# Splitting Q over all rows and queries at once, with DMAs that fill the stationary tiles by halves

## The chip, the cores and the metric

The kernel runs on one core of a Trainium2 chip. The metric is the device time of one execution in microseconds (us); the time of the kernel before is the median of three runs. The engines are TensorE (PE, with its weight loads as PEld), VectorE (DVE), ScalarE (ACT), GpSimd (POOL) and SyncE (SP), which here issues the DMAs. SBUF is the memory on the chip that the engines read, PSUM the one that PE's products land in.

## The reference

```python
# q, k, v: 8 batches, 8 heads, 576 positions, 64 per head
scores = matmul(q, k^T) / 8;  scores = where(pos_q // 64 >= pos_k // 64, scores, -1e9)
attn = exp(scores - rowmax);  attn = attn / (sum(attn) + 1e-9)
x = heads side by side of matmul(attn, v)                       # 8 x 576 x 512
gate = sigmoid(sum over k of conv_w[k] * x shifted by k)        # 5 taps along the positions
x = (gate * (x @ w_val)) @ w_out
u = x + real(fft over positions, then over features of x)
un = (u - mean) / sqrt(var + 1e-6)
out = u + relu(un @ w_ch1) @ w_ch2                              # 512 -> 2048 -> 512
```

Inputs and outputs are 32-bit floats. The change concerns the first line only: the scores of q against k.

## The kernel before

PE multiplies numbers of a shorter format (fp32r). To come near to 32-bit results, an operand is split into two parts: `hi`, the number as a copy into an fp32r tile rounds it, and `lo`, the difference between the number and `hi`. A product is then hi*hi + hi*lo + lo*hi.

The first part of the kernel (about 720 us) does attention, gated convolution and the Fourier mix; the second part (`phase2`, to 1540 us) does the network of 2048 features in nine groups, with weights that DVE decodes at its beginning. The change is in the first part alone. It goes through 32 pairs of heads, four to a batch. The raw tiles `qraw` and `kraw` hold a pair transposed: rows 0 to 63 are the 64 features of head 0, rows 64 to 127 those of head 1, and the 576 columns are positions. A pair has nine score blocks, i = 0 to 8: blocks 0 to 7 are 128 queries of one head (head i mod 2, queries 128 * (i // 2) and on, keys up to there), block 8 is the last 64 queries of both heads at once, in two pieces of 320 and 256 keys.

For blocks 0 to 7 the product needs only two matmuls (L405, L407). The first multiplies a stationary tile that holds q's hi in the 64 rows of the head and q's lo in the other 64 rows (`QQ[p][h]`) with a tile that holds k's hi twice (`KK[p][h]`, copied there by four DMAs of L368): hi*hi + lo*hi in one pass over 128 rows. The second multiplies `QZ`, q's hi with zeros in the other head's rows, with `KL`, k's lo: hi*lo. Block 8 takes three matmuls (mm3) with `QDH` and `QDL`, whose diagonal quarters hold the two heads' last 64 queries.

`split(p)` makes these tiles. Its stages run one to a block, beside the blocks of the pair before: `k_hi` (ACT, L57), then `k_dup` (DMAs, L368), `k_lo` (POOL, L363) and `q_hi` of head 0 (ACT, L63), then `q_lo` of head 0 (DVE, L345, which reads one half of the rows and writes the other) and `q_hi` of head 1, then `q_lo` of head 1 and two `d_hi` (ACT, L351), then two `d_lo` (DVE, L355). `spread(p, g)` copies a half of the queries of each head's hi into `QZ` (L383). The Q and K tiles of a pair are double buffered, `QDH` and `QDL` too; a `QZ` is held once and filled by halves: half 0 (blocks 0 to 3) behind block 4 of the pair before, half 1 (blocks 4 to 7) behind its block 8. The raw tiles come from a pool of three, of which a pair takes two.

After a block's product, DVE takes the row maximum (L427) and ACT the exponential with its sum (L440, `PB`), PE transposes it (L497), ACT copies it out (L502, `PTa`, `PTb`) and PE multiplies with v (L519). Beside that run the convolution's taps and gate (DVE L550, ACT L63), the Fourier products (L158 to L160) and the copies that split their operands. The loop `for n in range(NU + LT + LA)` writes one block per turn, with lags for the steps behind it; a scheduler then reorders the instructions of each engine, and each engine works through its own list in order. All DMAs spoken of here stand in one list, SP's.

Of the kernel before, what the change touches and what calls it, by code (L numbers as in the profile page):

```python
# [17 lines left out]
def kernel(  # L18
# [81 lines left out]
    def phase1():  # L100
        with ExitStack() as c1:
            kp = c1.enter_context(tc.tile_pool(name="kp", bufs=2))
            raw_p = c1.enter_context(tc.tile_pool(name="raw", bufs=3))
            sm = c1.enter_context(tc.tile_pool(name="sm", bufs=6))
            pa = c1.enter_context(tc.tile_pool(name="pa", bufs=1))
            px, pv, pg, pool = (c1.enter_context(tc.tile_pool(name=f"p{n}", bufs=1)) for n in "xvgz")
# [4 lines left out]

            make_identity(nc, ident)

            QDH = [pa.tile([P, P], F32R, name=f"QDH{i}") for i in range(2)]
            QDL = [pa.tile([P, P], F32R, name=f"QDL{i}") for i in range(2)]

            QZ = [[pa.tile([P, 256], F32R, name=f"QZ{h}{g}") for g in range(2)] for h in range(2)]
            PB = [pa.tile([P, 128 * (i // 2 + 1)], F32, name=f"PB{i}") for i in range(NB)]
            PTa = pa.tile([P, 2, 2, 256], F32, name="PTa")
            PTb = pa.tile([P, 2, 5, 320], F32, name="PTb")  # L120
# [184 lines left out]


            NPAIR = B * NP
            qraw, kraw, QQ, KK, KP, KL, VV = {}, {}, {}, {}, {}, {}, {}

            def load(p):  # L310
                if p >= NPAIR:
# [15 lines left out]
            def split(p):  # L327
                if p >= NPAIR:
                    return
                rs = [slice(0, 64), slice(64, 128)]  # L330

                QQ[p] = [kp.tile([P, D], F32R, tag=f"Q{h}", name=f"Q{h}") for h in range(2)]
                KK[p] = [kp.tile([P, S], F32R, tag=f"K{h}", name=f"K{h}") for h in range(2)]
                KP[p] = kp.tile([P, S], F32R, tag="KP", name="KP")
                KL[p] = kp.tile([P, S], F32R, tag="KL", name="KL")
                qq, kk, kh, kl = QQ[p], KK[p], KP[p], KL[p]
                dh, dl = QDH[p % 2], QDL[p % 2]

                def q_hi(h):
                    r = rs[h]  # L340
                    scaled(4, qq[h][r, :], qraw[p][r, 0:D], 0.125)

                def q_lo(h):
                    r = rs[h]
                    nc.vector.scalar_tensor_tensor(  # L345
                        out=qq[h][rs[1 - h], :], in0=qraw[p][r, 0:D], scalar=0.125,
                        in1=qq[h][r, :].bitcast(F32), op0=ALU.mult, op1=ALU.subtract)

                def d_hi(h):
                    r = rs[h]  # L350
                    nc.scalar.activation(out=dh[r, r], in_=qraw[p][r, D:S], func=AF.Copy, scale=0.125)  # L351

                def d_lo(h):
                    r = rs[h]
                    nc.vector.scalar_tensor_tensor(  # L355
                        out=dl[r, r], in0=qraw[p][r, D:S], scalar=0.125,
                        in1=dh[r, r].bitcast(F32), op0=ALU.mult, op1=ALU.subtract)
# [12 lines left out]
                def both(*f):  # L370
                    return lambda: [g() for g in f]

                return Chain(k_hi, both(k_dup, k_lo, lambda: q_hi(0)), both(lambda: q_lo(0), lambda: q_hi(1)),
                             both(lambda: q_lo(1), lambda: d_hi(0), lambda: d_hi(1)),
                             both(lambda: d_lo(0), lambda: d_lo(1)))

            def spread(p, g):

                if p >= NPAIR:
                    return  # L380
                for h in range(2):
                    r = slice(64 * h, 64 * h + 64)
                    nc.sync.dma_start(out=QZ[h][g][r, :].bitcast(F32),  # L383
                                      in_=QQ[p][h][r, 256 * g:256 * g + 256].bitcast(F32))

            sums, scs, maxs = {}, {}, {}

# [2 lines left out]
            def sc_tile(n):  # L390

                sc_at[0] += 1
                if n < NS and sc_at[0] % 5 > 2:
                    return ps_m.tile([P, D], F32, tag="m", name="sc")
                return ps_sc.tile([P, D], F32, tag="sc", name="sc")

            def emit_qk(n):
                p, i = divmod(n, NB)
                if i < 8:

                    h, L = i % 2, P * (i // 2 + 1)
                    w = max(256, L)
                    m = slice(P * (i // 2), P * (i // 2) + P)
                    t = sc_tile(n)
                    nc.tensor.matmul(t[:, 0:w], QQ[p][h][:, m], KK[p][h][:, 0:w], start=True, stop=False)  # L405
                    z = slice(P * (i // 2 % 2), P * (i // 2 % 2) + P)
                    nc.tensor.matmul(t[:, 0:w], QZ[h][i // 4][:, z], KL[p][:, 0:w], start=False, stop=True)  # L407
                    scs[n] = [(t[:, 0:L], 0, L)]
                    return

                sc = []
                for k0, w in ((0, 320), (320, 256)):
                    t = sc_tile(n)
                    mm3(t[:, 0:w], QDH[p % 2], QDL[p % 2], KP[p][:, k0:k0 + w], KL[p][:, k0:k0 + w], True, True)
                    sc.append((t[:, 0:w], k0, w))
                scs[n] = sc

# [412 lines left out]
            prepared = [0]  # L830
            load(0)
            nc.gpsimd.memset(PB[8][:, S:640], 0.0)
            for t in QDH + QDL + QZ[0] + QZ[1]:
                nc.gpsimd.memset(t.bitcast(F32), 0.0)
            split(0).run()
            spread(0, 0)
# [25 lines left out]
            for n in range(NU + LT + LA):  # L862
                if n == N1:
                    now[0] = 0
                p, i = divmod(n, NB)
# [22 lines left out]
                m = n - LT - LA  # L888
# [298 lines left out]
```

## Time and profile before

| | |
|---|---|
| median of 3 runs | 1539.53 us (1539.19 to 1540.07) |
| the profiled execution | 1541.68 us; its span, first to last instruction, 1539.9 |
| PE busy | 1464.1 us (95%), 8300 matmuls |
| DVE busy | 910.4 us (59%), 1894 instructions |
| ACT busy | 696.1 us (45%), 1770 instructions |
| POOL busy | 391.0 us (25%), 352 instructions |
| DMA queue of SP | 23.8% of the 16 engines' span, 108.78 MB |
| granted TensorE clock | 0.987 of full speed |

The busy shares are means over stages with different limits, so they are read by stretch: the first 60 us, the pair loop up to about 650 us, and the second part, in which PE has nearly all of the time. A row that ends in brackets tells how long the engine had stood idle before the instruction, and which instruction released it.

### The profile page before, as it was taken

Reading aid. Unit: us, or ns where it says so; the run is one execution under the profiler, and the core shown is the slowest. Engines: PE = TensorE matmul, PEld = TensorE weight load, DVE = VectorE, ACT = ScalarE, POOL = GpSimd, SP = SyncE. Lnnn points to the kernel's source line nnn. Section 1 sums busy time; section 2 is a strip of 40 time slices with the busy share of each in tenths; the row PEclk is TensorE's granted clock in tenths of the full one; section 3 lists DMA queues with packets and bytes.
Section 4 is the critical chain, followed back from the end, with each engine's and each line's share of the span. In section 5 each row is a group of like instructions: output and inputs, shape, how many; then the busy total and the mean of one; then the engine's idle time right before and its main releaser. Section 6 shows DMA issues by size and latency. Waiting matters only on the chain.

```text
span 1539.9 us, 22720 instructions
## 1 busy us (share of the span) xinstructions
PE 1464.1 (95%) x8300; PEld 1216.1 (79%) x8300; DVE 910.4 (59%) x1894; ACT 696.1 (45%) x1770; POOL 391.0 (25%) x352
## 2 busy tenths in 40 slices
PE   5799999999999999998888999999999999999998
PEld 4567888788888888886667888888888888888887
DVE  8888897979797989779995222222322222322212
ACT  6878777787868686734443211112121211212110
POOL 3433232323232333235434110111111201111100
PEclk9899999999999999999999999999999999999999
DMA  7444343333343433122541001010101001010000
GB/s 219 129 140 125 101 114 93 109 97 105 90 114 93 122 94 99 56 86 92 178 146 68 1 21 35 1 55 1 55 1 52 3 0 55 0 55 1 28 0 28
DMA packets 86624, 110.23 MB, mean 72 GB/s; under 512 B 8944, under 2 KB 60144, under 8 KB 86512
## 3 DMA queue, kind: packets, MB, share of 16 engines
q1 hardware_dynamic: 86512, 108.78, 23.8%
q8 instruction: 65, 1.06, 0.3%
q14 instruction: 47, 0.39, 0.1%
HBM read 62.61 MB, written 18.87 MB: 53 GB/s over the span
## 4 chain that ended last, share of the span: by engine, by line
PE 67%; DVE 20%; issue 6%; ACT 5%; POOL 1%; DMA 1%; SPq 0%; DVEq 0%; ACTq 0%; POOLq 0%
PE o L1079 8%; PE o L1077 8%; PE o L1078 8%; PE psh L1060 8%; PE psh L1059 8%; PE psh L1061 8%; PE av L519 4%; PE pt L497 3%; DVE mx L427 3%; DVE gate L550 2%; PE sc L405 2%; PE psx L158 2%; PE psx L160 2%; DVE st L76 2%; PE psx L159 2%
## 5 line engine op out<-in xcount | busy, mean ns | idle before, releaser
L1065 DVE SCALAR_TENSOR_TENSOR hl<-psh,hh 128x512 fp32r<-128x512 f32 x144 | 99.2, 689 | 397.8 <-ACT hh L1064 397.8
L1064 ACT ACTIVATE hh<-psh 128x512 fp32r<-128x512 f32 x144 | 85.8, 596 | 493.6 <-PE psh L1061 493.6
L1079 PE MATMUL o<-hl,W2H 128*128 128x512 f32 x576 | 226.4, 394 | 17.0 <-DVE hl L1065 17.0
L1061 PE MATMUL psh<-UTH,W1L 128*128 128x512 f32 x576 | 225.1, 391 | 1.2 <-POOL W1L L973 1.1
L1077 PE MATMUL o<-hh,W2H 128*128 128x512 f32 x576 | 225.7, 392 | 0.0
L1078 PE MATMUL o<-hh,W2L 128*128 128x512 f32 x576 | 225.6, 392 | 0.0
L1059 PE MATMUL psh<-UTH,W1H 128*128 128x512 f32 x576 | 224.9, 390 | 0.3 <-ACT W1H L972 0.3
L1060 PE MATMUL psh<-UTL,W1H 128*128 128x512 f32 x576 | 224.5, 390 | 0.0
L440 ACT ACTIVATE PB<-sc,mx 128x128 f32<-128x128 f32 (+4 forms) x320 | 167.2, 525 | 40.7 <-DVE mx L427 35.7
L427 DVE TENSOR_REDUCE mx<-sc 128x1 f32<-128x128 f32 (+4 forms) x320 | 147.9, 473 | 1.9 <-PE sc L160 0.2
L497 PE MATMUL pt<-ident,PB 128*128 128x128 f32 x800 | 140.6, 280 | 5.2 <-ACT XF L474 2.5
L1079 PEld LDWEIGHTS o<-hl,W2H 128*128 128x128 f32 x576 | 108.8, 189 | 44.2 <-DVE hl L1065 21.8
L550 DVE SCALAR_TENSOR_TENSOR gate<-XF,cw,gate 128x575 f32<-128x575 f32 (+3 forms) x128 | 132.5, 1035 | 2.9 <-ACT gate L63 2.1
L1061 PEld LDWEIGHTS psh<-UTH,W1L 128*128 128x128 f32 x576 | 108.4, 188 | 25.2 <-POOL W1L L973 2.5
L1059 PEld LDWEIGHTS psh<-UTH,W1H 128*128 128x128 f32 x576 | 108.6, 189 | 23.5 <-ACT W1H L972 0.7
L1078 PEld LDWEIGHTS o<-hh,W2L 128*128 128x128 f32 x576 | 109.1, 189 | 22.9
L1077 PEld LDWEIGHTS o<-hh,W2H 128*128 128x128 f32 x576 | 108.8, 189 | 22.9 <-ACT hh L1064 0.2
L1060 PEld LDWEIGHTS psh<-UTL,W1H 128*128 128x128 f32 x576 | 108.4, 188 | 22.5
L405 PE MATMUL sc<-K,Q 128*128 128x256 f32 (+2 forms) x256 | 94.5, 372 | 31.9 <-ACT PB L440 21.0
L497 PEld LDWEIGHTS pt<-ident,PB 128*128 128x128 f32 x800 | 100.8, 143 | 18.0 <-ACT PTb L502 9.9
L1088 POOL TENSOR_TENSOR U<-o,U 128x512 f32<-128x512 f32 x32 | 40.3, 1290 | 273.9 <-DVE o L1086 273.9
L502 ACT COPY PTb<-pt 128x512 f32<-128x512 f32 (+1 forms) x192 | 92.2, 500 | 21.7 <-PE pt L497 20.5
(187 smaller groups left out, 3019.2 us busy)
## 6 DMA issues: line engine op xcount, KB each, us to landing
K<-KP SPq DMA_DIRECT2D x128, 144.0 KB, 2.5
rw<-in_w_ch SPq DMA_DIRECT2D x32, 512.0 KB, 3.9
VV<-in_v SPq DMA_DIRECT2D x32, 320.0 KB, 3.3
qraw<-in_q SPq DMA_DIRECT2D x32, 288.0 KB, 3.1
kraw<-in_k SPq DMA_DIRECT2D x32, 288.0 KB, 3.0
out<-U SPq DMA_DIRECT2D x36, 256.0 KB, 2.0
QZ<-Q SPq DMA_DIRECT2D x128, 64.0 KB, 2.2
u_d<-XA SPq DMA_DIRECT2D x16, 289.0 KB, 2.2
```

Of the source, the lines that this page charges most:

```text
L405: nc.tensor.matmul(t[:, 0:w], QQ[p][h][:, m], KK[p][h][:, 0:w], start=True, stop=False)
L427: nc.vector.reduce_max(out=mx[:, j:j + 1], in_=t, axis=AX.X, negate=one)
L440: nc.scalar.activation(out=PB[i][:, k0:k0 + w], in_=t, func=AF.Exp, bias=nm, accum_out=su[:, i + j:i + j + 1])
L497: nc.tensor.transpose(ps[:, j, :], PB[i][:, (j0 + j) * P:(j0 + j + 1) * P], ident)
L550: nc.vector.scalar_tensor_tensor(out=gate[c][:, s:S], in0=XF[:, 0:S - s], scalar=cw[:, c, 4 - s:5 - s], in1=gate[c][:, s:S], op0=ALU.mult, ...
L1059: nc.tensor.matmul(ps, W1H[f][:, c, :], UTH[g][:, c, :], start=(c == 0), stop=False)
L1060: nc.tensor.matmul(ps, W1H[f][:, c, :], UTL[g][:, c, :], start=False, stop=False)
L1061: nc.tensor.matmul(ps, W1L[f][:, c, :], UTH[g][:, c, :], start=False, stop=(c == 3))
L1065: nc.vector.scalar_tensor_tensor(out=l, in0=ps, scalar=0.0, in1=h.bitcast(F32), op0=ALU.max, op1=ALU.subtract)
L1077: nc.tensor.matmul(po[t], W2H[e][:, c], h, start=(e == 0), stop=False)
L1078: nc.tensor.matmul(po[t], W2L[e][:, c], h, start=False, stop=False)
L1079: nc.tensor.matmul(po[t], W2H[e][:, c], l, start=False, stop=(e == NF - 1))
```

## The change

All rows and all 576 columns of `qraw` are split by one ACT instruction (`q_hi`) and one DVE instruction (`q_lo`) into one tile `QHL`, hi in its first half and lo in its second; rows stay where they are. What has to stand in other rows is carried there by DMAs: `q_last` copies the last 64 queries into `QD` (two DMAs), and `spread` fills, per head and half of the queries, `QQ[h][g]`: hi into the first and second 256 columns of the head's rows (one DMA that reads the source twice), lo into the first 256 columns of the other rows (one DMA). `QHL` and `QQ` are held once, and the raw pool has two tiles in place of three. The products read the same numbers as before.

```diff
-            raw_p = c1.enter_context(tc.tile_pool(name="raw", bufs=3))
+            raw_p = c1.enter_context(tc.tile_pool(name="raw", bufs=2))
...
-            QDH = [pa.tile([P, P], F32R, name=f"QDH{i}") for i in range(2)]
-            QDL = [pa.tile([P, P], F32R, name=f"QDL{i}") for i in range(2)]
-            QZ = [[pa.tile([P, 256], F32R, name=f"QZ{h}{g}") for g in range(2)] for h in range(2)]
+            QHL = pa.tile([P, 2, S], F32R, name="QHL")
+            QD = [pa.tile([P, 2, P], F32R, name=f"QD{i}") for i in range(2)]
+            QQ = [[pa.tile([P, 2, 256], F32R, name=f"QQ{h}{g}") for g in range(2)] for h in range(2)]
...
-                QQ[p] = [kp.tile([P, D], F32R, tag=f"Q{h}", name=f"Q{h}") for h in range(2)]
...
-                def q_hi(h):
-                    r = rs[h]
-                    scaled(4, qq[h][r, :], qraw[p][r, 0:D], 0.125)
-                def q_lo(h):
-                    r = rs[h]
-                    nc.vector.scalar_tensor_tensor(
-                        out=qq[h][rs[1 - h], :], in0=qraw[p][r, 0:D], scalar=0.125,
-                        in1=qq[h][r, :].bitcast(F32), op0=ALU.mult, op1=ALU.subtract)
...
+                def q_hi():
+                    nc.scalar.activation(out=QHL[:, 0, :], in_=qraw[p], func=AF.Copy, scale=0.125)
+                def q_lo():
+                    nc.vector.scalar_tensor_tensor(out=QHL[:, 1, :], in0=qraw[p], scalar=0.125,
+                                                   in1=QHL[:, 0, :].bitcast(F32), op0=ALU.mult, op1=ALU.subtract)
+                def q_last():
+                    for r in rs:
+                        nc.sync.dma_start(out=QD[p % 2][r, :, r].bitcast(F32), in_=QHL[r, :, D:S].bitcast(F32))
...
-                return Chain(k_hi, both(k_dup, k_lo, lambda: q_hi(0)), both(lambda: q_lo(0), lambda: q_hi(1)),
-                             both(lambda: q_lo(1), lambda: d_hi(0), lambda: d_hi(1)),
-                             both(lambda: d_lo(0), lambda: d_lo(1)))
+                return Chain(k_hi, both(k_dup, k_lo), wait, q_hi, q_lo, q_last)
             def spread(p, g):
...
+                c = slice(256 * g, 256 * g + 256)
                 for h in range(2):
-                    r = slice(64 * h, 64 * h + 64)
-                    nc.sync.dma_start(out=QZ[h][g][r, :].bitcast(F32),
-                                      in_=QQ[p][h][r, 256 * g:256 * g + 256].bitcast(F32))
+                    nc.sync.dma_start(out=QQ[h][g][rs[h], :, :].bitcast(F32),
+                                      in_=QHL[rs[h], 0:1, c].bitcast(F32).to_broadcast([64, 2, 256]))
+                    nc.sync.dma_start(out=QQ[h][g][rs[1 - h], 0, :].bitcast(F32), in_=QHL[rs[h], 1, c].bitcast(F32))
...
-                    m = slice(P * (i // 2), P * (i // 2) + P)
+                    m = slice(P * (i // 2 % 2), P * (i // 2 % 2) + P)
...
-                    nc.tensor.matmul(t[:, 0:w], QQ[p][h][:, m], KK[p][h][:, 0:w], start=True, stop=False)
-                    nc.tensor.matmul(t[:, 0:w], QZ[h][i // 4][:, z], KL[p][:, 0:w], start=False, stop=True)
+                    q = QQ[h][i // 4]
+                    nc.tensor.matmul(t[:, 0:w], q[:, 0, m], KK[p][h][:, 0:w], start=True, stop=False)
+                    nc.tensor.matmul(t[:, 0:w], q[:, 1, m], KL[p][:, 0:w], start=False, stop=True)
```

(`wait` is a stage that does nothing.) The lines of the kernel after stand some ten to twenty lower in number: L430 is L440 of before, L417 is L427, L492 is L502.

The order of ACT's instructions in the loop, before, at the first pair of a batch: the exponentials of block 7 (`PB_124`) and block 8 (`PB_125`, two pieces) with what stands around them.

```order
L63 ACTIVATE gate_143<-XF_128,cw 128x576
L502 COPY PTa<-pt 128x128
L63 ACTIVATE Q_4863<-qraw 64x512
L440 ACTIVATE PB_124,su<-sc,mx 128x512
L57 CAST KP<-kraw 128x576
L351 ACTIVATE QDH_110<-qraw 64x64
L502 COPY PTa<-pt 128x2x128
L440 ACTIVATE PB_125,su<-sc,mx 128x320
L440 ACTIVATE PB_125,su<-sc,mx 128x256
```

And the same place after, where the two blocks are `PB_123` and `PB_124`.

```order
L63 ACTIVATE gate_142<-XF_127,cw 128x576
L492 COPY PTa<-pt 128x128
L430 ACTIVATE PB_123,su<-sc,mx 128x512
L57 CAST KP<-kraw 128x576
L492 COPY PTa<-pt 128x2x128
L340 ACTIVATE QHL<-qraw 128x576
L430 ACTIVATE PB_124,su<-sc,mx 128x320
L430 ACTIVATE PB_124,su<-sc,mx 128x256
```

The copy of Q ahead of block 7's exponential is gone, and the copy into `QHL` stands ahead of block 8's, with the copy into `QDH` gone.

DVE's order at the same place, before: `XF` is the attention's result, which the convolution's copies on ACT wait for.

```order
L611 TENSOR_TENSOR GL_157<-GF_149,GH_153 128x580
L450 TENSOR_SCALAR su<-su 128x4
L345 SCALAR_TENSOR_TENSOR Q_4862<-qraw,Q_4862 64x512
L540 TENSOR_TENSOR XF_128<-av,XF_128 128x320
L451 RECIPROCAL re<-su 128x4
L588 SCALAR_TENSOR_TENSOR gv_148<-gate_144,psv 128x288
```

And after.

```order
L440 TENSOR_SCALAR su<-su 128x4
L417 TENSOR_REDUCE mx<-sc 128x1
L601 TENSOR_TENSOR GL_156<-GF_148,GH_152 128x580
L441 RECIPROCAL re<-su 128x4
L530 TENSOR_TENSOR XF_127<-av,XF_127 128x320
L578 SCALAR_TENSOR_TENSOR gv_147<-gate_143,psv 128x288
```

The difference for Q no longer stands ahead of `XF`; the short steps on the sums (`su`, `re`) and the convolution's product (`gv`) stand around `XF` as before.

SP's order at the start of the kernel, before, from the copies of pair 0's K on; pair 1's Q was asked for three rows earlier.

```order
L368 DMA K_193<-KP 64x576 x2
L368 DMA K_194<-KP 64x576 x2
L383 DMA QZ_113<-Q_191 64x256
L383 DMA QZ_115<-Q_192 64x256
L383 DMA QZ_114<-Q_191 64x256
L383 DMA QZ_116<-Q_192 64x256
L317 DMA kraw<-in_k 128x576
L234 DMA XA<-in_w_val 128x1024
```

And after, from the same copies on.

```order
L359 DMA K_188<-KP 64x576 x2
L359 DMA K_189<-KP 64x576 x2
L348 DMA QD_110<-QHL 64x2x64 x2
L374 DMA QQ_112<-QHL 64x256
L372 DMA QQ_114<-QHL 64x2x256
L374 DMA QQ_114<-QHL 64x256
L372 DMA QQ_113<-QHL 64x2x256
L374 DMA QQ_113<-QHL 64x256
L372 DMA QQ_115<-QHL 64x2x256
L374 DMA QQ_115<-QHL 64x256
L318 DMA qraw<-in_q 128x576
L320 DMA kraw<-in_k 128x576
```

Pair 1's Q and K are now asked for behind all copies of pair 0's Q.

## Rows read from the trace of the kernel before

**Rows 1.** Busy time by stage (from:to, length, engines busy, clock, DMA, GB/s)

```profile
20.00:60.00 40.00, 29.38 (x158) 20.47 (x158) 37.05 (x85) 29.45 (x82) 19.97 (x22) 0.83 0.59 178
300.00:400.00 100.00, 97.47 (x739) 83.45 (x738) 85.14 (x218) 77.01 (x224) 32.24 (x33) 1.00 0.36 99
760.00:800.00 40.00, 34.70 (x141) 27.09 (x141) 40.00 (x55) 17.95 (x32) 16.27 (x12) 0.96 0.48 155
```

**Rows 2.** PE's waits from 140 to 640 us (total us, times, longest us)

```profile
PE sc L405 <- ACT PB L440: 13.0, 19, 1.4
PE rt L466 <- POOL XF L454: 2.1, 6, 0.4
```

**Rows 3.** Groups by line, whole run (busy us, mean ns, idle before and releaser)

```profile
L550 DVE SCALAR_TENSOR_TENSOR gate<-XF,cw,gate 128x575 f32<-128x575 f32 (+3 forms) x128 | 132.5, 1035 | 2.9 <-ACT gate L63 2.1
...
L345 DVE SCALAR_TENSOR_TENSOR Q<-qraw,Q 64x512 fp32r<-64x512 f32 x64 | 58.3, 910 | 12.2 <-ACT Q L63 10.6
...
L363 POOL TENSOR_TENSOR KL<-kraw,KP 128x576 fp32r<-128x576 f32 x32 | 49.7, 1553 | 47.9 <-ACT KP L57 47.9
...
L63 ACT ACTIVATE Q<-qraw 64x512 fp32r<-64x512 f32 x64 | 40.3, 629 | 11.3 <-PE sc L405 8.1 <-DMA qraw<-in_q 2.5
...
L57 ACT CAST KP<-kraw 128x576 fp32r<-128x576 f32 x32 | 21.7, 679 | 0.1
...
L351 ACT ACTIVATE QDH<-qraw 64x64 fp32r<-64x64 f32 x64 | 16.3, 255 | 0.6
...
L355 DVE SCALAR_TENSOR_TENSOR QDL<-qraw,QDH 64x64 fp32r<-64x64 f32 x64 | 15.4, 241 | 0.8
```

**Rows 4.** Instructions that read qraw: ns shortest/median/longest, and us from first to last

```profile
L345 DVE SCALAR_TENSOR_TENSOR Q<-qraw,Q x64: 684/687/1796, 4.4 to 612.3; 64x512 fp32r<-64x512 f32 x64
```

**Rows 5.** Issues of QZ, 200 to 620 us: ns to issue, us to landing

```profile
L383 SPq DMA_DIRECT2D QZ<-Q x82: 461/462/829, 205.0 to 615.1; - x82
...
DMA to landing us min/median/max: 1.9/2.3/3.7
```

**Rows 6.** Timeline 441 to 447 us: start us, duration us, engine, line, idle before

```profile
441.04 0.69 DVE L345 SCALAR_TENSOR_TENSOR Q<-qraw,Q 64x512 fp32r<-64x512 f32 x1
...
443.81 0.63 ACT L63 ACTIVATE Q<-qraw 64x512 fp32r<-64x512 f32 x1
444.46 0.69 ACT L440 ACTIVATE PB<-sc,mx 128x512 f32<-128x512 f32 x1
...
445.29 0.39 PE L405 MATMUL sc<-K,Q 128*128 128x256 f32 x1 [1.36 <-ACT PB L440]
...
445.85 0.36 ACT L502 COPY PTa<-pt 128x256 f32<-128x256 f32 x1
...
446.31 0.53 ACT L440 ACTIVATE PB<-sc,mx 128x320 f32<-128x320 f32 x1
...
446.99 0.39 PE L405 MATMUL sc<-K,Q 128*128 128x256 f32 x1 [0.17 <-ACT PB L440]
```

**Rows 7.** Timeline 399 to 405 us, another pair

```profile
399.25 0.39 PE L407 MATMUL sc<-KL,QZ 128*128 128x512 f32 x1
...
401.44 0.69 ACT L440 ACTIVATE PB<-sc,mx 128x512 f32<-128x512 f32 x1
...
403.89 0.53 ACT L440 ACTIVATE PB<-sc,mx 128x320 f32<-128x320 f32 x1
...
404.56 0.39 PE L405 MATMUL sc<-K,Q 128*128 128x256 f32 x1 [0.49 <-ACT PB L440]
```

**Rows 8.** Chain of waits at the start: start us, us, what

```profile
24.95 0.70 DVE Q L345
...
26.39 1.80 DVE Q L345
```

**Rows 9.** Timeline of the first 24 us: pair 1's K

```profile
10.24 0.52 SPq L317 DMA_DIRECT2D kraw<-in_k  x1
...
14.71 0.67 ACT L57 CAST KP<-kraw 128x576 fp32r<-128x576 f32 x1
```

More of the change, by code (lines that the diff above doesn't have):

```diff
@@ L307, in phase1 @@
             NPAIR = B * NP
-            qraw, kraw, QQ, KK, KP, KL, VV = {}, {}, {}, {}, {}, {}, {}
+            qraw, kraw, KK, KP, KL, VV = {}, {}, {}, {}, {}, {}
+            rs = [slice(0, 64), slice(64, 128)]
             def load(p):
@@ L329, in split @@
                     return
-                rs = [slice(0, 64), slice(64, 128)]
-                QQ[p] = [kp.tile([P, D], F32R, tag=f"Q{h}", name=f"Q{h}") for h in range(2)]
                 KK[p] = [kp.tile([P, S], F32R, tag=f"K{h}", name=f"K{h}") for h in range(2)]
@@ L335, in split @@
                 KL[p] = kp.tile([P, S], F32R, tag="KL", name="KL")
-                qq, kk, kh, kl = QQ[p], KK[p], KP[p], KL[p]
-                dh, dl = QDH[p % 2], QDL[p % 2]
-                def q_hi(h):
-                    r = rs[h]
-                    scaled(4, qq[h][r, :], qraw[p][r, 0:D], 0.125)
-                def q_lo(h):
-                    r = rs[h]
-                    nc.vector.scalar_tensor_tensor(
-                        out=qq[h][rs[1 - h], :], in0=qraw[p][r, 0:D], scalar=0.125,
-                        in1=qq[h][r, :].bitcast(F32), op0=ALU.mult, op1=ALU.subtract)
[L349 to L357, printed above, removed]
+                kk, kh, kl = KK[p], KP[p], KL[p]
+                def q_hi():
[6 more added lines that the diff above has]
+                        nc.sync.dma_start(out=QD[p % 2][r, :, r].bitcast(F32), in_=QHL[r, :, D:S].bitcast(F32))
                 def k_hi():
@@ L402, in emit_qk @@
                     w = max(256, L)
-                    m = slice(P * (i // 2), P * (i // 2) + P)
+                    m = slice(P * (i // 2 % 2), P * (i // 2 % 2) + P)
                     t = sc_tile(n)
-                    nc.tensor.matmul(t[:, 0:w], QQ[p][h][:, m], KK[p][h][:, 0:w], start=True, stop=False)
-                    z = slice(P * (i // 2 % 2), P * (i // 2 % 2) + P)
-                    nc.tensor.matmul(t[:, 0:w], QZ[h][i // 4][:, z], KL[p][:, 0:w], start=False, stop=True)
+                    q = QQ[h][i // 4]
+                    nc.tensor.matmul(t[:, 0:w], q[:, 0, m], KK[p][h][:, 0:w], start=True, stop=False)
+                    nc.tensor.matmul(t[:, 0:w], q[:, 1, m], KL[p][:, 0:w], start=False, stop=True)
                     scs[n] = [(t[:, 0:L], 0, L)]
@@ L413, in emit_qk @@
                     t = sc_tile(n)
-                    mm3(t[:, 0:w], QDH[p % 2], QDL[p % 2], KP[p][:, k0:k0 + w], KL[p][:, k0:k0 + w], True, True)
+                    mm3(t[:, 0:w], QD[p % 2][:, 0], QD[p % 2][:, 1], KP[p][:, k0:k0 + w], KL[p][:, k0:k0 + w], True, True)
                     sc.append((t[:, 0:w], k0, w))
@@ L832, in phase1 @@
             nc.gpsimd.memset(PB[8][:, S:640], 0.0)
-            for t in QDH + QDL + QZ[0] + QZ[1]:
+            for t in QD + [QQ[h][g][rs[1 - h], 1, :] for h in range(2) for g in range(2)]:
                 nc.gpsimd.memset(t.bitcast(F32), 0.0)
```

## The prediction

> **What bounds the kernel now.** I read the busy time by stage first. From 20 to 60 us TensorE (PE) is busy 29 of 40 us and VectorE (DVE) 37: the start belongs to DVE, which decodes the first weights beside the attention of the first pairs of heads. From 300 to 400 us PE is busy 97.47 of 100 us, DVE 85 and ScalarE (ACT) 77: there PE is the bound, with 2.5% left. From 760 to 800 us DVE is busy all 40 us, decoding the weights of the second part [rows 1]. The reader is to see three stages with two different limits. Next, PE's waits between 140 and 640 us, where the pair loop runs evenly: 13.0 us for an exponential on ACT (nineteen times, the longest 1.4) and 2.1 us for a POOL copy: 15.1 us in 500 [rows 2]. Everything the change can win in the loop is inside that. The 32 pairs are 8 batches of 4; six of the batches fall in these 500 us, so each has some 2.5 us of it. Then I read one such wait event by event, below.
>
> The instruction order of every engine after the last pair's scores is the same in both kernels, and PE and DVE wait for each other there without a gap that the change could use. I take it that whatever is won or lost up to about 640 us is carried unchanged to the end.
>
> **The change, part by part.** PE multiplies the same tiles in the same number; its cost is zero but for waits.
>
> DVE loses, per pair, two differences of 64x512 (L345, mean 910 ns) and two of 64x64 (L355, 241 ns): 2.30 us. It gains one difference of 128x576. No such one stands in the trace with these operands; the nearest are the taps L550, the same operation over 128 partitions and 572 to 575 columns, mean 1035 ns. I take that: 1.27 us less a pair, 40.5 us over 32 pairs [rows 3]. The bounds come from the spread of L345, 684 to 1796 ns [rows 4]: at 0.77 us (684 x 576/512) the pair saves 1.53, at 1.8 us it saves 0.50.
>
> ACT loses two 64x512 copies (629 ns) and two 64x64 (255 ns), 1.77 us, and gains one of 128x576. KP is a copy of that size, 679 ns: 1.09 us less a pair, 35 us in all [rows 3].
>
> That L345 goes from 684 to 1796 ns is in [rows 4]. The Trainium skill, page "SBUF — State Buffer", section "Who interferes with whom", gives a reason: a VectorE instruction with two SBUF inputs and a GpSimd instruction that reads SBUF exclude each other, and the later one waits for the whole of the other. The spread agrees with it. The rule speaks against one long difference: the K difference on POOL (L363, 1553 ns [rows 3]) starts when KP ends, and q_lo comes about 1.06 us later (a PTa copy and q_hi in between), so by that rule up to 0.5 us of each q_lo may be blocked, 16 us of the 40.5. The sum would lose about 1 us by it, as little of that DVE time is on the path.
>
> SP issues 17 DMAs a pair in place of 11. A small one takes 0.462 us [rows 5], so 2.8 us more of a pair's 20 us; the queue has room. Bytes between SBUF tiles grow from 256 to 832 KB a pair, about 29 GB/s on 99, and the DMA share from 0.36 [rows 1] to about 0.47. I cost both at nothing except where something waits for a landing. Three such waits are new. The first product of a pair needs QQ, and its copies are issued behind the products of block 4 of the pair before, five blocks or some 11 us ahead: hidden. QD is read last in a pair: hidden, even were its 256-byte pieces slow. The third is q_hi, which must not overwrite QHL before the second half of the previous pair has been copied out of it. It is queued on ACT in front of the exponentials of the double block (i = 8), for which PE waits. That one counts.
>
> **The loop.** The wait of 1.36 us, once a batch, is in [rows 6]. A DVE difference of Q (441.04, 0.69) stands in front of XF, for which ACT's XH and gate wait; then ACT's own copy of Q (443.81, 0.63) stands in front of the exponential of block 7 (444.46), and PE waits for that one until 445.29. Both are gone in the new order: this exponential comes 0.69 + 0.63 = 1.32 us earlier. But q_hi now stands between it and the exponential of block 8. Before, that one came 446.31 - 445.15 = 1.16 us after block 7's ended; now KP 0.68 + PTa 0.36 + q_hi 0.69 = 1.73 us. It starts at 443.14 + 0.69 + 1.73 = 445.56 in place of 446.31, so the product at 446.99 moves by 0.75 us, not by 1.32: a new wait is late next.
>
> In another pair of the batch PE waits 0.49 us for block 8's exponential at 404.56 [rows 7]. Block 7's products end at 399.64. The later of the two second-half DMAs is issued 0.5 us after that and lands 1.9 to 3.7 us later, 2.3 at the median [rows 5]: at 402.4 with a median landing, at 403.8 with the worst. The exponential of block 7 is 0.6 us earlier without ACT's Q; then its 0.69, KP and PTa put q_hi's turn at 402.6. So it does not wait at the median, and with the worst landing it waits 1.2 us. Before, ACT worked 1.76 us without a gap between the two exponentials (402.13 to 403.89); now KP, a PTa copy or two and q_hi make 1.73 to 2.1 us, after a start 0.6 us earlier. So block 8's exponential stays near 403.5 at the median. I take zero here, between +0.7 (worst landing: q_hi ends at 404.5, not 403.89) and -0.49.
>
> The POOL copy, 2.1 us in six waits or 0.35 a batch, itself follows work in DVE's queue; with a shorter queue I count 0.3 of it. Sum: 1.05 us a batch, and with the uneven batches at the ends 5.2 of them: **-5.5 us**. Bounds: -15 (all the idle time goes) and, as a rival, a loss.
>
> **The start.** Up to 150 us nine pairs are split, 9 x 1.27 = 11.5 us of DVE. How much is on the path? The chain shows 0.70 and 1.80 us for Q at 24.95 and 26.39 [rows 8] for one pair; one new difference costs about 1.04 there: 1.5 us. Some three pairs of the nine have both on the path: -4.5 us, and ACT's share adds 0.5. Against this, pair 1 is loaded later. The raw pool holds two tiles in place of three, so its loads stand on SP behind all copies of pair 0. Its K was issued at 10.24 us and KP began at 14.71 [rows 9]. Now seven more DMAs stand ahead of that K (six more copies of pair 0, and pair 1's own load of Q), at 0.46 us each [rows 5]: K is issued 3.2 us later, at 13.4, and KP follows at about 17.9. The next weight load stands behind it too. In that time DVE has the weights and pair 0 to work on, so about half stays: +1.5 us. Start: **-3.5 us**, between -11.5 (all of DVE's saving counts) and +3 (the whole delay counts and nothing is won).
>
> **The sum** is -9.0 us. The profiled execution took 1541.7 us (span 1539.9 and 1.8 around it), so it would be 1532.7; the median of the runs is 1539.5, 2.2 below it, and there the same saving gives **1530.5 us**.
>
> **Rivals.**
> (a) The relief is hidden. PE is busy 97.5% of the loop, and both engines that are relieved run beside it; if q_hi's new place also eats the 0.75 us, and the late pair 1 eats the start's gain, the rest is within 3 us: 1537 to 1542. For it: the wait that replaces the removed one; against it: DVE's 37 of 40 us at the start.
> (b) Slower: q_hi waits for the copies. Two DMAs, the later one twice the size of QZ, behind a V load; if it lands 3.3 us after its issue, 1 us over the median, q_hi waits from its turn about 0.8 us. From 2.5 us on this decides. Three pairs in four have q_hi in front of block 8; one of the three has slack, so 16 pairs x 0.8 = 13 us are lost, the loop's 5.5 mostly with them (one batch place in two): 1539.5 - 3.5 - 2 + 13 = 1547. For it: the worst landing of 3.7; against: the median of 2.3.
> (c) The start is DVE's alone and the loop's idle time all goes: -11.5 + 1.5 - 11 = -21: 1518. For it: DVE at 93% from 20 to 60 us; against: PE and ACT are busy 29.4 of the 40 us there too [rows 1] and have chains of their own.
> (d) The lower price of a full-width difference does not come, because it is blocked each time at 1.8 us: the pair saves 0.50 us, and the start wins 1.5 instead of 5; with the loop at -4 that is 1535.5.
>
> **Chances.** Forecast 0.48 (1525 to 1536), (d) 0.06, (a) 0.17, (b) 0.19, (c) 0.10. 0.2% is 3.1 us, about what measurements of this kernel tell from no change. Faster by more: the forecast, (c) and most of (d), 0.61; within: (a) and a little of (d), 0.20; slower: (b), 0.19. The range has to leave out at most 0.2: 1519 cuts half of (c), 1545 cuts most of (b), so **1519 to 1545**.
>
> **What would show it.** DVE's Q group at 32 instructions of 0.8 to 1.2 us, some 33 us in all, and ACT's at 0.69. PE's wait for the exponentials in the loop down from 13.0 to about 8 us, with the 1.4 us cases replaced by 0.7 us ones in front of the second product. PE busy from 300 to 400 us above 98.5. The batch shorter by about 1 us. KP of pair 1 at about 18 us. I am wrong if ACT shows q_hi idle before it on a DMA landing by more than 5 us in all (then (b)), if the batch is as long as before (then (a)), or if the stages after 660 us do not keep their length.

## The result, and the profile after

The changed kernel takes 1526.42 us (median of four runs, 1523.36 to 1528.32) against 1539.36: a ratio of 0.9916, 95% interval 0.9897 to 0.9936, or 12.9 us less. A second series gave 0.9908 (0.9895 to 0.9920). The forecast was 1530.5, 9.0 us less. The profiled execution took 1526.26 us, its span 1524.5.

The busy time by stage, columns as in [rows 1]:

```profile
20.00:60.00 40.00, 26.24 (x130) 16.80 (x130) 31.82 (x74) 24.57 (x70) 18.98 (x22) 0.79 0.66 177
300.00:400.00 100.00, 98.62 (x764) 86.57 (x766) 80.59 (x208) 75.78 (x217) 33.65 (x32) 1.00 0.53 137
760.00:800.00 40.00, 34.06 (x139) 26.71 (x138) 40.00 (x54) 17.76 (x32) 17.64 (x14) 0.96 0.40 132
```

PE is up to 98.62 of 100 us in the loop, DVE down by 4.5, ACT by 1.2. The first stage does not look like a gain: every engine is busy less of it than before, PE 26.24 of 40 us in place of 29.38, at a granted clock of 0.79 of full speed in place of 0.83. In the loop the granted clock is 1.00 in both. DMA share in the loop is 0.53, where 0.47 was reckoned.

PE's waits from 140 to 640 us, which answer to [rows 2]:

```profile
PE sc L396 <- ACT PB L430: 8.0, 9, 1.7
```

8.0 us are left of 15.1, so 7.1 us went. But the loop got 13.5 us shorter. The rest is in the waits of PE's weight loads, which no row ahead of the prediction shows. Before:

```profile
PEld sc L405 <- ACT PB L440: 19.0, 27, 1.6
PEld pt L497 <- ACT PTb L502: 6.7, 19, 0.7
...
PEld rt L466 <- POOL XF L454: 4.3, 6, 0.7
...
PEld rt L466 <- POOL KL L363: 1.9, 5, 0.4
```

After:

```profile
PEld sc L396 <- ACT PB L430: 13.0, 18, 1.9
...
PEld pt L487 <- ACT PTb L492: 1.3, 6, 0.2
...
PEld rt L456 <- POOL XF L444: 1.1, 5, 0.2
```

These four waits sum to 31.9 us before and the three to 15.4 after. A weight load that comes late pushes its matmul, but not all of the delay shows as the matmul's idle time. At the place of [rows 6] the weight load shows a longer wait than the 1.36 us of its product:

```profile
445.29 0.19 PEld L405 LDWEIGHTS sc<-K,Q 128*128 128x128 f32 x1 [1.59 <-ACT PB L440]
```

And the product itself is listed with 0.39 us there, with 0.28 where it did not wait (436.46 below). So a part of PE's waiting is counted as busy. From the first product of pair 10 to that of pair 30, with the same matmuls in between, the time fell from 408.7 to 394.9 us: PE's idle time by 5.9 us, its busy time by 7.9 (396.1 to 388.2).

The instructions of the split, with columns as in [rows 3], and the spread of q_lo as in [rows 4]:

```profile
L343 DVE SCALAR_TENSOR_TENSOR QHL<-qraw,QHL 128x576 fp32r<-128x576 f32 x32 | 24.0, 749 | 6.3 <-ACT QHL L340 6.3
...
L340 ACT ACTIVATE QHL<-qraw 128x576 fp32r<-128x576 f32 x32 | 22.2, 694 | 10.9 <-DMA QQ<-QHL 3.2 <-DMA K<-KP 3.1 <-DMA u_d<-XA 2.4
```

```profile
L343 DVE SCALAR_TENSOR_TENSOR QHL<-qraw,QHL x32: 727/748/880, 4.3 to 599.8; 128x576 fp32r<-128x576 f32 x32
```

A full-width difference takes 0.749 us, not 1.035, and none took over 0.88.

Where the time went, by the start of each pair's first product (us, read off the timelines; later kernels below in the same way, as differences from the kernel before):

| | pair 2 | pair 10 | pair 31 | second part's first product | span |
|---|---|---|---|---|---|
| before | 35.98 | 200.06 | 627.40 | 709.3 | 1539.9 |
| changed | +12.8 | +0.2 | -13.3 | -14.8 | -15.4 |
| changed, second series | +11.8 | +0.4 | -12.5 | -15.3 | -16.8 |

So the start gave nothing on balance (pair 2 is late by 12.8 us, pair 10 is level), the loop from pair 10 to 31 gave 13.5 us in 21 pairs, 2.6 a batch, and 2.1 us came behind it, 1.5 of them before the second part. In the loop the step is always at the same place: the first products of pairs 10, 14, 18, 22 and 26 gained 2.0 us each on that of the pair before, that of pair 30 gained 1.8.

The place of [rows 6] once more. First the kernel before, lines that were not shown (columns as there):

```profile
437.65 3.33 POOL L756 TENSOR_TENSOR XA<-XA 128x580 f32<-128x580 f32 x2 [1.50 <-DVE XA L756]
...
438.02 1.67 DVE L611 TENSOR_TENSOR GL<-GF,GH 128x580 fp32r<-128x580 f32 x1
...
439.61 1.40 DVE L450 TENSOR_SCALAR su<-su 128x4 f32<-128x4 f32 x1
...
439.79 0.39 PE L405 MATMUL sc<-K,Q 128*128 128x512 f32 x1
...
441.75 0.49 DVE L540 TENSOR_TENSOR XF<-av,XF 128x320 f32<-128x320 f32 x1
```

And the changed kernel at the same batch:

```profile
430.13 0.15 DVE L440 TENSOR_SCALAR su<-su 128x4 f32<-128x4 f32 x1
...
430.24 3.34 POOL L746 TENSOR_TENSOR XA<-XA 128x580 f32<-128x580 f32 x2 [1.39 <-DVE sc L415]
...
432.29 0.45 DVE L530 TENSOR_TENSOR XF<-av,XF 128x320 f32<-128x320 f32 x1
...
432.48 0.39 PE L396 MATMUL sc<-K,QQ 128*128 128x512 f32 x1
...
434.18 0.69 ACT L430 ACTIVATE PB<-sc,mx 128x512 f32<-128x512 f32 x1
...
436.46 0.28 PE L396 MATMUL sc<-K,QQ 128*128 128x256 f32 x1
...
436.66 0.69 ACT L340 ACTIVATE QHL<-qraw 128x576 fp32r<-128x576 f32 x1 [0.37 <-DMA QQ<-QHL]
...
437.26 0.51 ACT L430 ACTIVATE PB<-sc,mx 128x320 f32<-128x320 f32 x1
...
437.91 0.39 PE L396 MATMUL sc<-K,QQ 128*128 128x256 f32 x1
```

Before, the short step on the sums (L450, 128x4) took 1.40 us: it began at 439.61 and ended at 441.01, as POOL's two additions (L756) ended at 440.98. In the new order it stands ahead of POOL's additions and takes 0.15. That, with Q's difference gone, brings `XF` from 1.96 us behind block 7's first product (439.79) to 0.19 ahead of it (432.48), and the exponential of block 7 from 4.67 us behind it to 1.70: 2.97 us earlier. PE's product at 436.46 no longer waits. It is the same in all six batches from pair 10 to pair 30: before, the step on the sums took 1.39 or 1.40 us and ended 0.02 to 0.03 us behind POOL's additions, block 7's exponential came 4.66 or 4.67 us behind the product, and PE waited 1.36 to 1.39 us at the next pair's first product; in the changed kernel the step took 0.30 us at most (from 140 to 640 us), the exponential came after 1.64 to 1.70, and that wait is gone. q_hi waits in its stead: its row, with 0.37 us of idle time before it, stands between the exponentials of blocks 7 and 8. Block 8's first exponential came 6.52 us behind block 7's product before (446.31) and 4.78 after (437.26).

ACT's waits in front of q_hi, 140 to 640 us (which engine or queue, total us, times, longest):

```profile
ACT QHL L340 <- DMA QQ<-QHL: 3.2, 3, 1.7
...
ACT QHL L340 <- DMA K<-KP: 3.1, 2, 1.7
ACT QHL L340 <- DMA u_d<-XA: 2.4, 3, 1.0
```

8.7 us in all. The wait of rival (b) is there: each of these eight waits ended 0.15 to 0.18 us after the last copy out of `QHL` had landed, whichever transfer the view names. Those last copies landed 3.0 to 4.3 us after their issue.

### The profile page after: what moved, and what is told of

Read it like the earlier page. It is cut to its first block, busy times and chain, and to the rows that moved or that the text cites. A ratio compares the mean times of both kernels' runs of the same rounds, so it can differ in the third digit from the quotient of the medians.

```text
span 1524.5 us, 22867 instructions
## 1 busy us (share of the span) xinstructions
PE 1449.9 (95%) x8300; PEld 1213.1 (80%) x8300; DVE 859.1 (56%) x1798; ACT 666.4 (44%) x1674; POOL 393.1 (26%) x350
## 4 chain that ended last, share of the span: by engine, by line
PE 80%; DVE 10%; DMA 3%; issue 3%; ACT 3%; POOL 1%; SPq 1%; DVEq 0%; ACTq 0%; POOLq 0%
PE o L1069 8%; PE o L1067 8%; PE o L1068 8%; PE psh L1050 8%; PE psh L1051 8%; PE psh L1049 8%; PE av L509 6%; PE pt L487 5%; PE sc L396 3%; PE sc L397 2%; PE psx L160 2%; PE psx L162 2%; PE psx L161 2%; DVE st L76 2%; PE psv L160 2%
## 5 line engine op out<-in xcount | busy, mean ns | idle before, releaser
L430 ACT ACTIVATE PB<-sc,mx 128x128 f32<-128x128 f32 (+4 forms) x320 | 167.0, 524 | 47.9 <-DVE mx L417 40.8
L487 PE MATMUL pt<-ident,PB 128*128 128x128 f32 x800 | 139.1, 279 | 11.3 <-ACT PTb L492 4.2
L417 DVE TENSOR_REDUCE mx<-sc 128x1 f32<-128x128 f32 (+4 forms) x320 | 148.0, 473 | 2.7
L1051 PEld LDWEIGHTS psh<-UTH,W1L 128*128 128x128 f32 x576 | 108.1, 188 | 25.5 <-POOL W1L L963 2.9
L1068 PEld LDWEIGHTS o<-hh,W2L 128*128 128x128 f32 x576 | 109.3, 190 | 22.9
L396 PE MATMUL sc<-K,QQ 128*128 128x256 f32 (+2 forms) x256 | 92.6, 363 | 26.1 <-DMA QQ<-QHL 13.0
L492 ACT COPY PTb<-pt 128x512 f32<-128x512 f32 (+1 forms) x192 | 92.8, 501 | 31.2 <-PE pt L487 29.9
```

Source lines behind the costliest of these rows:

```text
L396: nc.tensor.matmul(t[:, 0:w], q[:, 0, m], KK[p][h][:, 0:w], start=True, stop=False)
L417: nc.vector.reduce_max(out=mx[:, j:j + 1], in_=t, axis=AX.X, negate=one)
L430: nc.scalar.activation(out=PB[i][:, k0:k0 + w], in_=t, func=AF.Exp, bias=nm, accum_out=su[:, i + j:i + j + 1])
L487: nc.tensor.transpose(ps[:, j, :], PB[i][:, (j0 + j) * P:(j0 + j + 1) * P], ident)
L1051: nc.tensor.matmul(ps, W1L[f][:, c, :], UTH[g][:, c, :], start=False, stop=(c == 3))
L1068: nc.tensor.matmul(po[t], W2L[e][:, c], h, start=False, stop=False)
```

## The experiments

The changed kernel itself ran once more beside the first ones (the second series above).

> The changed kernel once more, beside the kernel before and the variants below on one chip. Both theories: ratio 0.990 to 0.994, some 1524 to 1529 us. The stages as in the first profile: first product of pair 2 about 12 us later than before, of pair 10 level with before, of pair 31 about 13 us earlier.

It came out so: 1524.99 us.

**1. The load of pair 1 ahead of the copies of pair 0.**

```diff
             split(0).run()
+            load(1)
             spread(0, 0)
             spread(0, 1)
             load_v(0)
-            load(1)
```

> The changed kernel, but pair 1's Q and K are asked for ahead of most copies of pair 0's Q. Theory A: the late pair 1 costs the start about as much as the shorter DVE queue gives it (12 us each, seen at pairs 2 and 10), so the first product of pair 1 comes at 20 to 22 us in place of 29.4, and 4 to 10 us of it stay to the end: 1516 to 1522 us, ratio 0.985 to 0.989. Theory B: the start is bound by DVE's weight decoding, which fills the time whether pair 1 is late or not: within 2 us of the changed kernel, 1524 to 1529.

Measured: 1528.26 us, ratio 0.9935 (0.9918 to 0.9951), 3.3 us above the changed kernel beside it (1524.99); the two intervals just touch, and its six runs spread from 1525.02 to 1533.74. Pair 1's first product came at 25.8 us, 3.6 earlier. But two kernels below ask for pair 1 behind pair 0's copies, as the changed one does, and have that product at 25.8 (lo_split) and 24.0 (qd_late), so it is not shown that the earlier request moved it. Pair 2's came only 1.9 earlier, and from pair 4 on the kernel is behind the changed one, 4.0 us at pair 10. The scheduler reordered other work with it. Theory A did not come; the time lies in the range given for theory B, but not within its 2 us of the changed kernel. Asking earlier did not help the start.

**2 and 3. The empty stage, put into the kernel before and taken out of the changed one.**

```diff
-                return Chain(k_hi, both(k_dup, k_lo, lambda: q_hi(0)), both(lambda: q_lo(0), lambda: q_hi(1)),
+                return Chain(k_hi, both(k_dup, k_lo), wait, lambda: q_hi(0), both(lambda: q_lo(0), lambda: q_hi(1)),
```

> The kernel before, with one empty stage between the K difference on POOL and the two-part split of Q, as the changed kernel has it. Theory A: part of the loop's gain is that Q's differences no longer meet POOL's K difference: DVE's mean for L345 falls from 910 to about 690-720 ns (some 13 us of DVE), the loop shortens by 3 to 6 us: 1533 to 1537 us, ratio 0.996 to 0.998. Theory B: the meeting costs nothing on the path, the gain is the number of instructions removed: within 1 us of before, ratio 0.999 to 1.001.

```diff
-                return Chain(k_hi, both(k_dup, k_lo), wait, q_hi, q_lo, q_last)
+                return Chain(k_hi, both(k_dup, k_lo, q_hi), q_lo, q_last)
```

> The changed kernel without the empty stage: q_hi runs beside the K difference, so q_lo meets it. Theory A: q_lo's mean rises from 749 ns to 1100 or more (12 us of DVE or more), 3 to 6 us of the gain are lost: 1529 to 1533 us, ratio 0.993 to 0.996. Theory B: within 2 us of the changed kernel, ratio 0.990 to 0.994.

Measured: the first 1542.54 us, ratio 1.0024 (1.0015 to 1.0033); the second 1530.68, ratio 0.9956 (0.9944 to 0.9968). Q's differences, in the first with columns as in [rows 3], in the second as in [rows 4]:

```profile
L345 DVE SCALAR_TENSOR_TENSOR Q<-qraw,Q 64x512 fp32r<-64x512 f32 x64 | 54.6, 853 | 13.4 <-ACT Q L63 11.7
```

```profile
L343 DVE SCALAR_TENSOR_TENSOR QHL<-qraw,QHL x32: 719/738/1737, 4.5 to 602.4; 128x576 fp32r<-128x576 f32 x32
```

Neither settles what the meeting with POOL's K difference costs. In the kernel before, the stage takes the differences of Q that overlap it from 10 of 64 to 2, but seven long ones now overlap POOL's additions (`XA`), so the mean falls only from 910 to 853 ns, and the kernel is slower. In the changed kernel none of the 32 q_lo overlaps the K difference, and without the stage only two do: the meeting that theory A is about was hardly brought about. The time came out where A had it, but not for its reason: the median of q_lo is 738 ns, its mean 795, and the loop from pair 10 to pair 31 gives 12.5 us (+3.7 to -8.8), nearly the changed kernel's 13.5. The loss is there at pair 10 already, so it is one of the start.

**4 to 6. The merged instructions undone, one engine at a time.** In q_hi and in q_lo:

```diff
-                    nc.scalar.activation(out=QHL[:, 0, :], in_=qraw[p], ...)
+                    for r in rs: nc.scalar.activation(out=QHL[r, 0, :], in_=qraw[p][r, :], ...)
...
-                    nc.vector.scalar_tensor_tensor(out=QHL[:, 1, :], in0=qraw[p], ...)
+                    for r in rs: nc.vector.scalar_tensor_tensor(out=QHL[r, 1, :], in0=qraw[p][r, :], ...)
```

> The changed kernel, with q_hi done as two ACT instructions of 64x576, one per head: ACT gets back some 0.68 us a pair (22 us in all), everything else as in the changed kernel. Theory A (the loop's gain is mostly DVE's shorter queue in front of XF): it costs only what q_hi's place in front of block 8's exponential takes, 1 to 3 us: 1526 to 1529 us, ratio 0.991 to 0.994. Theory B (ACT's shorter queue gives the gain): half or more of the 13 us is lost, 1531 to 1537 us, ratio 0.995 to 0.999.

> The changed kernel, with q_lo done as two DVE instructions of 64x576, one per head: DVE gets back some 0.75 us a pair (24 us in all). Theory A: 4 to 9 us of the gain are lost, 1529 to 1534 us, ratio 0.994 to 0.997. Theory B: within 2 us of the changed kernel, ratio 0.990 to 0.993.

> The changed kernel with both splits: what is left of the change is the layout, the DMAs that carry the rows, the empty stage and the two raw tiles. Theories A and B: nearly all of the gain comes from the merged instructions, so 1532 to 1538 us, ratio 0.996 to 1.000. Theory C (the gain comes from the new layout and the later place of the split, not from fewer instructions): ratio 0.994 or lower.

Measured: q_hi alone 1528.54 us, ratio 0.9931 (0.9919 to 0.9943); q_lo alone 1531.45, 0.9950 (0.9933 to 0.9966); both 1549.55, 1.0061 (1.0049 to 1.0073). One by one their times are those of theory A: about 2 us lost for ACT, 5 for DVE (against the changed kernel's 1526.4). But A is about the loop, and there the places do not fit it: from pair 10 to 31 hi_split still gives 10.7 us and lo_split 12.3, of the changed kernel's 13.5 (12.9 in the second series); most of lo_split's loss, 3.7 us, is in the start, as with no_wait_stage. So neither instruction alone carries the loop's gain. Both together cost 23, and the kernel is slower than before: the new layout with its DMAs is a loss without the merged instructions. The trace of that kernel shows what comes together:

```profile
427.61 0.68 ACT L340 ACTIVATE QHL<-qraw 64x576 fp32r<-64x576 f32 x1 [1.97 <-DMA QQ<-QHL]
```

```profile
448.04 1.39 DVE L440 TENSOR_SCALAR su<-su 128x4 f32<-128x4 f32 x1
...
454.40 0.39 PE L396 MATMUL sc<-K,QQ 128*128 128x256 f32 x1 [2.03 <-ACT PB L430]
```

```profile
PE sc L396 <- ACT PB L430: 21.5, 16, 2.1
...
DVE QHL L343 <- ACT QHL L340: 11.1, 8, 2.1
```

q_hi's first half waits 1.97 us for copies out of `QHL`, ahead of ACT's copy of `XF` and the gate, and q_lo's halves wait for q_hi in DVE's queue (11.1 us from 140 to 640). And the step on the sums stands behind `GL` and beside POOL's additions again, as before the change: 1.39 or 1.40 us in five batches, and 6.4 us after the start of each PE waits 2.0 to 2.1 us for an exponential at a pair's first product, 10 us in all, where the loop from pair 10 to 31 is 18 us longer than the changed kernel's. In hi_split and lo_split the step takes 0.53 and 1.01 us at most from 140 to 640, and no wait at a first product is over 0.2. PE's waits for the exponentials are 21.5 us, more than before the change.

**7 and 8. q_hi behind the exponentials.** `QD` is held once and copied with the second half, with two raw tiles (7, "qd_late") and with three, for which it makes room (8, "raw3").

```diff
-            QD = [pa.tile([P, 2, P], F32R, name=f"QD{i}") for i in range(2)]
+            QD = [pa.tile([P, 2, P], F32R, name="QD0")] * 2
...
-                return Chain(k_hi, both(k_dup, k_lo), wait, q_hi, q_lo, q_last)
+                return Chain(k_hi, both(k_dup, k_lo), wait, q_hi, q_lo)
             def spread(p, g):
+                if g:
+                    for r in rs:
+                        nc.sync.dma_start(out=QD[0][r, :, r].bitcast(F32), in_=QHL[r, :, D:S].bitcast(F32))
```

> The changed kernel with the pool of three raw tiles again; to make room, QD is held once, and its two copies are issued with those of the second half, behind block 8. Pair 1's Q is asked for ahead of pair 0's copies again, its K still behind them. Theory A (the start loses about 12 us by the late pair 1): pair 1's first product at 20 to 24 us in place of 29, and 3 to 10 us gained at the end: 1515 to 1522 us, ratio 0.985 to 0.989. Theory D (pair 1 is late because eleven to thirteen copies at 0.6 us stand on SP ahead of its K copies, and the asking order matters little, as load_first suggests): first product of pair 1 at 26 us or later, total within 3 us of the changed kernel: 1522 to 1528, ratio 0.989 to 0.993.

> The changed kernel with two raw tiles as it has, but QD held once and copied behind block 8, as in raw3. In the order of ACT this puts q_hi behind block 8's exponentials in every pair, where the changed kernel has it in front of them in three pairs of four. Theory E (raw3 gained 10 us because q_hi, with its wait for the landing of QQ, no longer stands in front of the exponentials that PE waits for): PE's waits for exponentials from 140 to 640 us fall from 8 to 1 to 3 us, and the time comes to 1515 to 1519 us, ratio 0.984 to 0.988, as raw3. Theory F (the third raw tile gained it, by earlier loads): waits stay near 7 to 8 us and 1522 to 1527 us, ratio 0.989 to 0.993.

Measured: raw3 1516.25 us, ratio 0.9852 (0.9837 to 0.9866); qd_late 1519.06, 0.9863 (0.9846 to 0.9879). raw3 hit the time of theory A, but pair 2 was as late as ever (+13.6) and pair 10 level (-0.1): of the 10.2 us by which its profiled execution is shorter than the changed kernel's, 7.5 came in the loop from pair 10 to 31 and the rest behind it. In its order ACT's q_hi stands behind block 8's exponentials, and qd_late, which has that order with the two raw tiles, tells which of the two it was. PE's waits in it:

```profile
PE sc L396 <- ACT PB L430: 1.3, 1, 1.3
```

And ACT's in front of q_hi:

```profile
ACT QHL L340 <- DMA QD<-QHL: 0.7, 2, 0.5
...
ACT QHL L340 <- DMA K<-KP: 0.3, 1, 0.3
```

1.3 us in place of 8.0, and ACT idles 1.0 us in front of q_hi in place of 8.7. In 17 of the changed kernel's 32 pairs q_hi stands straight ahead of block 8's exponentials, here in none. Theory E holds. With these matmuls the loop has next to nothing left to win: from pair 10 to pair 30 PE is busy 388.5 of 388.6 us, in raw3 as well. The third raw tile is worth the 2.4 us of pair 10 in the profiles; the two intervals overlap, so no more is said of it.

**9 and 10. The start.** As raw3, with the copies of pair 0's second half behind pair 1's load (9), and besides with the K copies of pairs 0 to 2 issued by ACT (10).

```diff
-            spread(0, 1)
             load_v(0)
             load(1)
+            spread(0, 1)
...
-                            nc.sync.dma_start(out=kk[h][r, :].bitcast(F32), in_=kh[rs[h], :].bitcast(F32))
+                            (nc.scalar if p < 3 else nc.sync).dma_start(out=kk[h][r, :].bitcast(F32), ...)
```

> As raw3, and at the start the copies of pair 0's second half are issued behind the load of pair 1, so that pair 1's K is asked for six DMAs, some 3.6 us, earlier. Theory A (the late loads of pair 1 cost the start): pair 1's first product 3 us sooner than in raw3 (25.0), 2 to 4 us gained at the end, ratio 0.982 to 0.984. Theory D (DVE's weights and the copies on SP limit the start, the order of asking matters little): pair 2 and later within 1 us of raw3, ratio 0.984 to 0.987.

> As raw3_half_late, but the four K copies of each of the pairs 0, 1 and 2 are issued by ACT, not by SP, so that SP's list at the start is twelve DMAs of 0.6 us shorter. Theory D (the copies standing in one list on SP set the start): the first products of pairs 0 to 2 come 2 to 6 us sooner than in raw3_half_late (11.8, 25.5 and 47.6), and 3 us or more stay to the end: 1510 to 1513 us, ratio 0.979 to 0.983. Theory G (the start is set by the chain of ACT, DVE and PE through the weights and the first pairs, not by SP): from pair 3 on within 1.5 us of raw3_half_late, 1514 to 1518 us, ratio 0.984 to 0.987.

Measured: 1515.53 us, ratio 0.9839 (0.9824 to 0.9853), and 1516.35, 0.9852 (0.9831 to 0.9874). In 9 pair 1's first product came at 25.5, where raw3 had 25.0; theory D's time holds, though pair 2 came 2.0 sooner, where it allowed 1. In 10 the first products of pairs 0 to 2 came 0.8, 1.8 and 4.5 us sooner than in 9 (D had said 2 to 6), but the median did not follow: its interval holds that of 9, and the time is theory G's. The profiled execution of 10 is the fastest of its four and that of 9 the slowest, so the difference between their places is uncertain.

The kernels in the table's terms:

| | pair 2 | pair 10 | pair 31 | second part | span |
|---|---|---|---|---|---|
| before_wait | -0.1 | -3.2 | +2.4 | 0.0 | -1.1 |
| load_first | +10.9 | +4.2 | -6.8 | -9.4 | -10.7 |
| no_wait_stage | +13.0 | +3.7 | -8.8 | -11.3 | -11.4 |
| hi_split | +13.5 | -0.1 | -10.8 | -13.8 | -13.2 |
| lo_split | +11.6 | +3.9 | -8.4 | -9.4 | -10.3 |
| both_split | +12.5 | +3.7 | +8.5 | +6.4 | +5.0 |
| qd_late | +14.7 | +2.3 | -18.7 | -21.6 | -22.9 |
| raw3 | +13.6 | -0.1 | -21.1 | -24.1 | -25.6 |
| raw3_half_late | +11.6 | +0.3 | -20.6 | -23.1 | -24.7 |
| kdup_act | +7.1 | -3.3 | -24.2 | -25.8 | -27.6 |

## Why the prediction came out right, and where its steps did not

The time lay 4 us from the forecast, inside its range, on the side that was forecast. Two terms of the sum were mis-sized against each other: the loop by 8 us too small, the start by 3.5 too large. A further 2.1 us came behind the last pair's first product, where nothing was counted. That the sum came so near is in part luck.

**The loop: -5.5 reckoned, -13.5 measured.** The step "this exponential comes 0.69 + 0.63 = 1.32 us earlier" is the one that was mis-sized: it came 2.97 us earlier, since the step on the sums, with 1.40 us as long as Q's difference and copy together, went too. Block 8's exponential was reckoned to move by 0.75 us and moved by 1.74, so most of what is missing is at this place. The step on the sums stood in the order shown ahead of the prediction, but its duration was not looked up. The Trainium skill, page "SBUF — State Buffer", section "Who interferes with whom", says that a VectorE copy, cast or tensor_scalar in a two-port mode and a GpSimd instruction exclude each other until the one that came first has ended; the two ends at 441.01 and 440.98 agree with it. That the step matters is shown by both_split too, where its 1.40 us and the wait at the first product came back together. "Everything the change can win in the loop is inside" 15.1 us was wrong as a bound: raw3 wins 21.0 us from pair 10 to pair 31, and the weight loads' waits show why. A new wait at the second product, with q_hi ahead of it, was right in kind: eight of the nine waits that are left are at a pair's second product, 0.2 to 1.7 us each.

**The wait for the landing** was taken as zero at the second place, between +0.7 and -0.49. q_hi waited 8.7 us there and elsewhere, 1.7 at most, and its place in front of the exponentials cost about 7 us (experiments 7 and 8); what of that is the wait and what q_hi's own 0.69 us in front of them was not separated. Rival (b)'s mechanism was real at about half its price, and covered by a larger gain. The step that failed here is the landing, taken at its median of 2.3 us: where q_hi waited it took 3.0 to 4.3. Over all pairs the twofold copy shows:

```profile
L372 SPq DMA_DIRECT2D QQ<-QHL x84: 590/616/1211, 205.7 to 611.4; - x84
...
DMA to landing us min/median/max: 2.3/2.4/4.4
```

**The start: -3.5 reckoned, 0 measured at pair 10.** Pair 1 was late for the reason given: K asked for later, KP later still.

```profile
14.67 0.40 SPq L320 DMA_DIRECT2D kraw<-in_k  x1
...
18.54 0.66 ACT L57 CAST KP<-kraw 128x576 fp32r<-128x576 f32 x1
```

K was forecast at 13.4 and KP at 17.9. Reckoned was that half of the 3.2 us stays, +1.5; what came was +9.8 at pair 1's first product and +12.8 at pair 2's. Behind KP, four copies of K, two into `QD` and those into `QQ`, 0.6 us each, stand on SP; all that fill K and the first half of Q for pair 1 had landed by 27.1 us. But its first product came only at 29.4. In PE's list it stands behind transposes, and these waited for an exponential, which waited for DVE, where the row maximum stood behind steps on the weights:

```profile
26.16 1.67 DVE L55 CAST wv_h<-gv 128x512 fp32r<-128x512 f32 x1
...
27.75 0.14 DVE L419 TENSOR_REDUCE mx<-mx 128x1 f32<-128x2 f32 x1
...
27.92 0.53 ACT L430 ACTIVATE PB<-sc,mx 128x320 f32<-128x320 f32 x1 [1.25 <-DVE mx L419]
...
28.60 1.14 PE L487 MATMUL pt<-ident,PB 128*128 128x128 f32 x4 [2.54 <-ACT PB L430]
...
29.39 0.56 PE L396 MATMUL sc<-K,QQ 128*128 128x256 f32 x1
```

So the step "about half stays" left out both the length of SP's list behind KP and the work that the engines' new orders put ahead of the product. From pair 2 to pair 10 12.6 us came back; that DVE's shorter list gave them is argued, not shown. Experiments 1 and 9 show that the order of asking alone does not bring the delay of pair 2 back. With a shorter list on SP (10) pair 2 came 4.5 us sooner, in one execution each and without a gain in the median. What holds pair 2, the lower granted clock of that stage included, is open.

**DVE and ACT.** The pair saves 2.30 - 0.75 = 1.55 us of DVE, not 1.27; the lower bound's 0.77, worked out from L345's shortest, was the better price, and (d) is out: no q_lo was blocked long. That 16 us might be blocked by POOL's K difference, as the rule was weighed, did not come: no q_lo overlapped it, and the longest took 0.88. ACT's price, 0.68 for q_hi, was right at 0.694.

**The signs named.** PE's wait for the exponentials at about 8 us, PE over 98.5 from 300 to 400 us, and KP of pair 1 at about 18 came so. DVE's Q group is 24 us in all, not 33, and the waits at the second product go up to 1.7 us, not 0.7. The batch was 2.6 us shorter, not 1. The second part kept its length to 0.6 us (1.5 in the second series). The sign for (b), q_hi idle for more than 5 us, came too, without (b)'s time; as a sign it did not tell the two apart, since a wait and a gain can stand side by side.

**What stays open:** how the 18 us that both splits together cost the loop divide among these waits (q_hi's wait alone is not it: hi_split has 13.7 us of it put down to `QQ`, both_split 10.7), and the start.

## What to carry to other kernels

Where PE is busy 97% of a stage, its matmul rows do not bound what is to be won: the waits of the weight loads have to be read with them. When an order changes, look up the real duration of each instruction that stands ahead of the one PE waits for, short ones too: here a step on 128x4 numbers took 1.40 us beside POOL. A tile held once makes its writer wait for the copies out of it; put that writer behind the work that PE waits for, not ahead of it, which here was worth about 7 us more.

## What the runs showed of the hardware that was not expected

A difference over 128 rows and 576 columns took 0.748 us at the median and one over 64 rows of the same length 0.755 (both_split); for ACT's copy it is 0.688 and 0.683 (hi_split). At this size the rows cost nothing, and splitting by rows doubles the price. A step of 128x4 took 0.15 us alone and 1.40 beside POOL's additions. Issuing a copy between SBUF tiles took 0.46 us on SP for a 64x256 piece before, and 0.59 to 0.62 with the second copy in it and often for the plain ones among them after, so seventeen a pair hold SP for some 10 of 20 us.
